# Sums and parts of v and of the weights pinned to their steps, and the first two products of the next pair ahead of the three that end the pair in work

## The chip, the cores and the metric

The kernel runs on one core of a Trainium2 chip. TensorE (PE in the profile; its weight loads are PEld) multiplies, VectorE (DVE), ScalarE (ACT) and GpSimd (POOL) work beside it, and SyncE (SP) issues all DMAs. The metric is device time in microseconds (us) of one execution. Before the change the median of three runs is 2376.45 us (2374.65 to 2376.95).

## The reference

Channel attention on q, k and v of shape (4, 6080, 256), and then a gated layer without a second input on all 4 x 6080 tokens:

```python
qn = q / (norm(q, axis=1) + 1e-06)
kn = k / (norm(k, axis=1) + 1e-06)
s = kn.transpose(0, 2, 1) @ qn / tau        # 256 x 256 for each batch
a = softmax(s)                              # exp(s - max) / (sum + 1e-09)
x = (v @ a).reshape(24320, 256)
h = x @ w_in                                # 256 x 2048
g = h * sigmoid(1.702 * h)
return g @ w_out                            # 2048 x 256
```

## The kernel before

For each batch the attention matrix is folded into the input weights, so that v is multiplied by one matrix of 256 x 2048 that is new in each batch ("the weights"). The product of v and the weights is done by Strassen's scheme in Winograd's form, with seven block products in place of eight, called P0 to P6 here after the block of weights that each uses. That needs sums of blocks of v and of the weights ahead of the products, and sums of products after them. Each fp32 operand is split into a high and a low part (`split`, L81: a cast on ACT, then a subtraction on DVE), and each product is three matmuls: high x high, high x low, low x high.

**The stream.** The tokens of a batch lie in 12 chunks of up to 512 (half a chunk is 256 columns, in the last chunk 224). A chunk meets 8 pairs of 128-row blocks of the hidden layer. One pair is one *period*; the four batches have 384 of them. `Hidden` holds a pair, and its work has three pieces:

- `begin` (L541): P0 into half of one PSUM bank (`ps_x`), P4 into half of another (`ps_y`). ACT copies P0 out (`r1`, L553), and DVE adds it to P4 (`u2`, L554).
- `middle` (L556): P5 into `ps_y` and P3 into `ps_x`. P5 has to wait until DVE has read `ps_y` for `u2`. DVE then makes `r25` (L561) and adds it in `ps_y` (L563).
- `end` (L565): P1, P6 (`ps_x`) and P2 (`ps_y`). DVE adds `u2` to both banks (L569, L570), and `gate` (L576) runs the activation `g` from each bank (ACT, L581) and splits it into `gh` and `gl` (ACT L82, DVE L83).

`project` (L592) multiplies `gh` and `gl` by the output weights, six matmuls of up to 512 columns for each of the pair's two blocks. The list `late` holds it back, so that a period projects the pair that ended one period earlier. The banks for pairs come from a pool of four (`ps_h`), so a new pair takes the banks of the pair before the last.

**Order.** In the main loop TensorE's order is written by hand (`manual_schedule` for PE, L754). A period is, in TensorE's order: `end` of the pair before, `begin` of the new pair, a `project`, the side work of step 2s, `middle`, a `project`, the side work of step 2s + 1. All other engines run in order from queues whose order a scheduler decides by its own costs, as early as data and buffers allow. `with tc.issue_after(ins)` puts ACT's instructions of a block behind `ins` in ACT's queue; work of the block on other engines follows only through its data. `pinned` (L749) does so with `newest[0]`, the `r1` of the newest pair. Before the change only the preparation of q and k (`prep`) and the first piece of each weight conversion go through it.

**Side work** is given a step (`put`, `put0`, `put_w`). In a chunk that begins at step `at_v`, for the next chunk: `v_load` (three DMAs) at `at_v` + 3, `v_sums` (four additions, on POOL after the first chunks) at `at_v` + 6, and four `v_split` at `at_v` + 8, 10, 12 and 14. The parts of v (`vh`, `vl`) have two buffers, so the parts of the next chunk go where those of the chunk before were, and are free to be written once that chunk's last product has run. For the next batch, `prepare` of a unit of q and k every 4 steps (two splits and two squares on ACT, their low parts on DVE, sums on POOL), its scores three steps later, then norms, softmax (`softmax_a`, L358, with exp on ACT, L384) and, in the last chunk and the first steps of the next batch, for each of four groups `win_load`, `win_split`, `weights` (L431), `weight_sums` and `weight_split`.

A stage of some 62 us before the main loop does batch 0's attention. In the first 160 us the weights also have to be put together from 64-bit words.

Of the kernel before, what the change touches and what calls it, by code (L numbers as in the profile page):

```python
# [27 lines left out]
def channel_attention_then_glu(  # L28
# [27 lines left out]
    NF = DFF // P  # L56
# [121 lines left out]
    class Attention:  # L178
# [98 lines left out]
        def score(self, u, qs, ks):  # L277
            nt = self.units[u][1]
            start = 0 if self.alone else self.direct
            if u == start:  # L280
                self.s = [
                    ps_s.tile([P, 2 * C], F32, tag=f"s{i}", name=f"s{i}")
                    for i in range(NC2)
                ]
            steps = [(j, i) for j in range(nt) for i in range(NC2)]
            last = u == len(self.units) - 1
            if u < self.direct:
                for j, i in steps:
                    nc.tensor.matmul(
                        self.s[i][:, :C],  # L290
                        lhsT=ks[:, j, i * P : (i + 1) * P],
                        rhs=qs[:, j, :],
                        start=u == start and j == 0,
                        stop=last and j == nt - 1,
                    )
                return

            for j, i in steps:
                nc.tensor.matmul(  # L299
                    self.s[i],  # L300
                    lhsT=ks[:, j, 0, i * P : (i + 1) * P],
                    rhs=qs[:, j, :, :],
                    start=u == start and j == 0,
                    stop=False,
                    skip_group_check=True,
                )
            for j, i in steps:
                nc.tensor.matmul(  # L308
                    self.s[i][:, C:],
                    lhsT=ks[:, j, 1, i * P : (i + 1) * P],  # L310
                    rhs=qs[:, j, 0, :],
                    start=False,
                    stop=last and j == nt - 1,
                    skip_group_check=True,
                )
# [276 lines left out]
    def project(b, c, f, gh, gl):  # L592
        o, w = chunks[c]
        if f == 0:

            room = [(ps_s, f"s{i}") if (b, c) == (0, 1) else (ps_o, "o") for i in range(NC2)]
            po[b, c] = [p.tile([P, NCH], F32, tag=t, name="ps_o") for p, t in room]
        out = po[b, c]
        for d in range(NC2):
            ds = slice(d * P, (d + 1) * P)  # L600
            for n, (l, r) in enumerate(((wo_h, gh), (wo_h, gl), (wo_l, gh))):
                nc.tensor.matmul(  # L602
                    out[d][:, :w], lhsT=l[:, f, ds], rhs=r[:, :w],
                    start=f == 0 and n == 0, stop=f == NF - 1 and n == 2,
                )
        if f == NF - 1:
            for d in range(NC2):
                osb = op.tile([P, NCH], F32, tag="osb", name="osb")[:, :w]
                if d == 0:
                    nc.vector.tensor_copy(osb, out[d][:, :w])  # L610
                else:
                    nc.scalar.copy(osb, out[d][:, :w])
                dst = outT[d * P : (d + 1) * P, b * N + o : b * N + o + w]
                nc.sync.dma_start(dst, osb)
# [10 lines left out]
    at = Attention(0, nu)  # L625
    nxt = Attention(1, 4)
# [75 lines left out]
    def put0(s, fn, *a):  # L702
        start.setdefault(s, []).append((fn, a))
# [7 lines left out]
        11: ("out", 3), 12: ("in", 6), 14: ("in", 7), 16: ("out", 4),  # L711
        18: ("out", 5), 20: ("out", 6), 22: ("out", 7),
    }
    running = {}
    newest = {}

# [17 lines left out]

    wanted = {1: 8, 2: 16, 3: 22}
    for g, n in wanted.items():
        put0(n - 5, at.win_split, g)
        for i in range(NC2):
            put0(n - 4 + i, at.weights, g, i)
        put0(n - 3, at.weight_sums, g)  # L740
        put0(n - 2, at.weight_split, g, 0)
        put0(n - 2, at.weight_split, g, 1)


    late = []
    open_ = []
    WIDE = max(begun) + 4

    def pinned(fn, *a):  # L749
        with tc.issue_after(newest[0].ins):  # L750
            fn(*a)


    with tc.manual_schedule(engines={mybir.EngineType.PE}):  # L754
        for b in range(B):
            side = start if b == 0 else carried
            following = {}
            order = [(c, f) for c in range(NCHUNK) for f in range(NF // 2)]
            if b == 0:

                beside = [(c, f) for f in range(5) for c in range(2)]
                order[:NF] = beside + [(c, f) for c in range(2) for f in range(5, NF // 2)]

            def put(s, fn, *a):
                side.setdefault(s, []).append((fn, a))

            for c in range(2 if b == 0 else 1, NCHUNK + (b + 1 < B)):
                at_v = (c - 1) * NF
                bc = (b, c) if c < NCHUNK else (b + 1, 0)
                first_v = at_v + 3  # L770
                if b == 0 and c == 2:
                    first_v = 27
                put(first_v, v_load, *bc)
                late_v = max(at_v + 6, first_v + (1 if b == 0 and c == 2 else 3))
                put(late_v, v_sums, *bc)
                for n in range(4):
                    put(at_v + 8 + 2 * n if first_v == at_v + 3 else 29 + n // 2, v_split, *bc, n)
            if b + 1 < B:
                if b:
                    nxt = Attention(b + 1)  # L780
                held = {}

                def prep(u, nxt=nxt, held=held):
                    held[u] = nxt.prepare(u)

                def score(u, nxt=nxt, held=held):
                    nxt.score(u, *held.pop(u))

                first = 2 * NF + 3 if b == 0 else 20
                nd = nxt.direct  # L790
                for u in range(nu):
                    if u < nd:
                        put(WIDE + 2 * u, pinned, prep, u)
                        continue
                    at_u = first + 4 * (u - nd)
                    put(at_u - 4, nxt.fetched, u)
                    put(at_u, pinned, prep, u)
                    put(at_u + 3, score, u)
                e = first + 4 + 4 * (nu - nd)
                put(e, nxt.norms_a)  # L800
                put(e + 4, nxt.norms_b)
                put(e + 9, nxt.norms_c)
                put(e + 10, nxt.softmax_a)
                put(e + 13, nxt.softmax_c)
                put(e + 16, nxt.transposes)
                total = NCHUNK * NF
                for g in range(NG):

                    n = total - NF + 4 * g + 5
                    there = side if n < total else following  # L810
                    n -= 0 if n < total else total

                    def put_w(s, fn, *a, there=there):
                        there.setdefault(s, []).append((fn, a))

                    put(total - NF + 4 * g - 2, nxt.win_load, g)
                    put(total - NF + 4 * g + 2, nxt.win_split, g)
                    for i in range(NC2):
                        put_w(n + i, nxt.weights, g, i)
                    put_w(n + 1, nxt.weight_sums, g)  # L820
                    put_w(n + 2, nxt.weight_split, g, 0)
                    put_w(n + 2, nxt.weight_split, g, 1)

            def sides(s):
                for fn, a in side.get(s, ()):
                    fn(*a)

            for s, (c, fp) in enumerate(order):
                if b == 0 and 2 * s == WIDE:
                    wide[0] = 1  # L830
                if open_:
                    late.extend(open_.pop().end())
                h = Hidden(at, b, c, fp)
                open_.append(h)
                h.begin()
                if len(late) > 2:
                    project(*late.pop(0))
                sides(2 * s)
                h.middle()
                if len(late) > 2:  # L840
                    project(*late.pop(0))
                sides(2 * s + 1)
            carried = following
            if b + 1 < B:
                at = nxt
        late.extend(open_.pop().end())
        while late:
            project(*late.pop(0))
# [27 lines left out]
```

## Time and profile before

| | |
|---|---|
| median of three runs | 2376.45 us |
| the profiled execution | 2376.57 us |
| its span, first to last instruction | 2374.8 us |
| mean granted TensorE clock | 0.994 |
| TensorE busy in the slice 2300 to 2374 us | 71.27 of 74 us |
| HBM over the span | 49 GB/s |

The profiled execution stands 0.1 us over the median, and 1.8 us of it lie outside the span. TensorE is busy in nearly all of the 40 slices of the span, but its matmuls overlap: a matmul of 256 columns is shown as 0.28 us long, and the next starts 0.12 us after it. So the time that TensorE loses is read from the starts of its matmuls and from the idle time ahead of its weight loads, and not from its busy share.

### The profile page before, as it was taken

How to read it: one execution, taken by the hardware profiler on the slowest of the kernel's cores; microseconds unless marked ns; L12 is line 12 of the kernel's file. 1: busy time of each engine (PE TensorE's matmuls, PEld its weight loads, DVE VectorE, ACT ScalarE, POOL GpSimd, SP SyncE). 2: the span in 40 equal slices, each digit the busy share in tenths (PEclk: the TensorE clock that was granted, in tenths of full speed). 3: DMA queues.
4: the chain of work that ended last, by engine and by line, in shares of the span. 5: the costliest groups of instructions: out<-in, count | busy, mean ns of one | idle time of the engine just before them, and what ended most of it. 6: DMA issues, size and time to landing. Idle time of an engine off the chain costs nothing.

```text
span 2374.8 us, 36966 instructions
## 1 busy us (share of the span) xinstructions
PE 2266.9 (95%) x13712; PEld 2001.5 (84%) x13712; DVE 1667.0 (70%) x3347; ACT 1329.7 (56%) x2690; POOL 390.4 (16%) x396
## 2 busy tenths in 40 slices
PE   8899999999999999999999999999999999999999
PEld 7678888878888888888888888888888888888888
DVE  7887767766667777777666777777667666666665
ACT  6666665554555666555455666565546444544544
POOL 0013322200121332220011232222002100000000
PEclk9899999999999999999999999999999999999999
DMA  8222111100011211211010111211001000100100
GB/s 325 89 80 81 63 63 60 45 25 29 28 35 36 81 63 54 70 45 35 19 36 26 63 63 56 70 34 36 27 19 36 26 28 19 36 19 19 35 10 17
DMA packets 55204, 118.77 MB, mean 50 GB/s; under 512 B 6128, under 2 KB 20976, under 8 KB 55024
## 3 DMA queue, kind: packets, MB, share of 16 engines
q1 hardware_dynamic: 55024, 116.42, 14.6%
q8 instruction: 107, 1.75, 0.3%
q14 instruction: 73, 0.60, 0.1%
HBM read 89.39 MB, written 27.00 MB: 49 GB/s over the span
## 4 chain that ended last, share of the span: by engine, by line
PE 73%; DVE 12%; ACT 10%; issue 4%; DMA 1%; SPq 0%; ACTq 0%; DVEq 0%
PE ps_o L602 33%; PE ps_x L535 19%; PE ps_y L535 14%; DVE gl L83 3%; ACT vh L82 3%; PE s L299 3%; ACT g L581 2%; PE ps_w L448 2%; DVE ps_x L569 2%; DVE u L554 1%; PE s L308 1%; DVE vl L83 1%; DVE ps_y L570 1%; DVE wl L83 1%; ACT gh L82 1%
## 5 line engine op out<-in xcount | busy, mean ns | idle before, releaser
L83 DVE TENSOR_TENSOR gl<-g,gh 128x512 fp32r<-128x512 f32 (+1 forms) x768 | 567.3, 760 | 167.2 <-ACT gh L82 162.5
L602 PE MATMUL ps_o<-gl,wo_h 128*128 128x512 f32 (+1 forms) x1536 | 605.1, 394 | 0.8 <-DVE gl L83 0.7
L602 PE MATMUL ps_o<-gh,wo_h 128*128 128x512 f32 (+1 forms) x1536 | 605.9, 394 | 0.0
L602 PE MATMUL ps_o<-gh,wo_l 128*128 128x512 f32 (+1 forms) x1536 | 597.2, 389 | 0.0
L581 ACT ACTIVATE g<-ps_x 128x512 f32<-128x512 f32 (+1 forms) x384 | 227.6, 593 | 652.0 <-DVE ps_x L569 651.5
L82 ACT CAST gh<-g 128x512 fp32r<-128x512 f32 (+1 forms) x768 | 443.7, 627 | 4.3 <-PE ps_o L602 0.7
L535 PE MATMUL ps_x<-vh,wh 128*128 128x256 f32 (+1 forms) x1536 | 435.2, 283 | 5.4 <-DVE r L561 5.1
L535 PE MATMUL ps_x<-vl,wh 128*128 128x256 f32 (+1 forms) x1536 | 434.5, 283 | 1.5 <-DVE vl L83 1.5
L535 PE MATMUL ps_x<-vh,wl 128*128 128x256 f32 (+1 forms) x1536 | 434.6, 283 | 0.7 <-DVE wl L83 0.7
L535 PE MATMUL ps_y<-vh,wh 128*128 128x256 f32 (+1 forms) x1152 | 340.9, 296 | 87.0 <-DVE u L554 77.4
L569 DVE TENSOR_TENSOR ps_x<-ps_x,u 128x256 f32<-128x256 f32 (+1 forms) x384 | 163.9, 427 | 269.0 <-PE ps_x L535 266.9
L535 PEld LDWEIGHTS ps_y<-vh,wh 128*128 128x128 f32 x1152 | 219.8, 191 | 148.9 <-DVE u L554 123.2
L602 PEld LDWEIGHTS ps_o<-gh,wo_l 128*128 128x128 f32 x1536 | 290.2, 189 | 62.1
L535 PE MATMUL ps_y<-vh,wl 128*128 128x256 f32 (+1 forms) x1152 | 325.9, 283 | 2.6 <-DVE wl L83 2.6
L535 PE MATMUL ps_y<-vl,wh 128*128 128x256 f32 (+1 forms) x1152 | 325.7, 283 | 0.2 <-DVE vl L83 0.2
L602 PEld LDWEIGHTS ps_o<-gh,wo_h 128*128 128x128 f32 x1536 | 292.7, 191 | 34.4
L602 PEld LDWEIGHTS ps_o<-gl,wo_h 128*128 128x128 f32 x1536 | 292.4, 190 | 31.9 <-DVE gl L83 1.8
L535 PEld LDWEIGHTS ps_x<-vh,wh 128*128 128x128 f32 x1536 | 293.9, 191 | 26.2 <-DVE r L561 12.1
L535 PEld LDWEIGHTS ps_x<-vl,wh 128*128 128x128 f32 x1536 | 294.2, 192 | 12.8 <-DVE vl L83 1.7
L535 PEld LDWEIGHTS ps_x<-vh,wl 128*128 128x128 f32 x1536 | 294.3, 192 | 0.9 <-DVE wl L83 0.9
L554 DVE TENSOR_TENSOR u<-ps_y,r 128x256 f32<-128x256 f32 (+1 forms) x384 | 160.5, 418 | 151.6 <-ACT r L553 150.5
L581 ACT ACTIVATE g<-ps_y 128x512 f32<-128x512 f32 (+1 forms) x384 | 231.5, 603 | 0.4 <-DVE ps_y L570 0.4
(123 smaller groups left out, 2769.8 us busy)
## 6 DMA issues: line engine op xcount, KB each, us to landing
out_T<-osb SPq DMA_DIRECT2D x88, 256.0 KB, 2.2
raw_q<-in_q SPq DMA_DIRECT2D x33, 512.0 KB, 3.6
raw_k<-in_k SPq DMA_DIRECT2D x33, 512.0 KB, 4.6
v_raw<-in_vT SPq DMA_DIRECT2D x44, 256.0 KB, 2.7
v_raw<-in_vT SPq DMA_DIRECT2D x88, 128.0 KB, 2.8
win<-win SPq DMA_DIRECT2D x16, 512.0 KB, 3.3
raw_q<-in_q SPq DMA_DIRECT2D x6, 768.0 KB, 8.8
raw_k<-in_k SPq DMA_DIRECT2D x6, 768.0 KB, 9.8
```

The costliest lines, as they stand in the source:

```text
L82: ins = nc.scalar.copy(dst_hi, src)
L83: nc.vector.tensor_tensor(dst_lo, src, dst_hi.bitcast(F32), op=ALU.subtract)
L299: nc.tensor.matmul(self.s[i], lhsT=ks[:, j, 0, i * P : (i + 1) * P], rhs=qs[:, j, :, :], start=u == start and j == 0, stop=False, skip_gro ...
L308: nc.tensor.matmul(self.s[i][:, C:], lhsT=ks[:, j, 1, i * P : (i + 1) * P], rhs=qs[:, j, 0, :], start=False, stop=last and j == nt - 1, sk ...
L448: nc.tensor.matmul(ps, lhsT=l[:, j, ci], rhs=r[:, j, :], start=n == 0, stop=n == 3 * NC2 - 1,)
L535: nc.tensor.matmul(out, lhsT=l[:, wi, :], rhs=r[:, vi, : self.hw], start=first and n == 0, stop=last and n == 2, skip_group_check=True,)
L554: nc.vector.tensor_tensor(u2, self.y[:, 1], r1, op=ALU.add)
L569: nc.vector.tensor_tensor(self.x[:, 1], self.x[:, 1], self.u2, op=ALU.add)
L570: nc.vector.tensor_tensor(self.y[:, 0], self.y[:, 0], self.u2, op=ALU.add)
L581: nc.scalar.activation(g, ps, AF.Gelu_apprx_sigmoid)
L602: nc.tensor.matmul(out[d][:, :w], lhsT=l[:, f, ds], rhs=r[:, :w], start=f == 0 and n == 0, stop=f == NF - 1 and n == 2,)
```

## The change

It has two parts. `pinned` is now also laid around `v_sums`, `v_split`, `win_split`, `weight_sums` and `weight_split` in the main loop. And `begin` of the new pair is issued ahead of `end` of the pair before it, so that a period is P0, P4 of the new pair; P1, P6, P2 of the pair before; project; P5, P3; project.

```diff
+    def pinned(fn, *a):
+        with tc.issue_after(newest[0].ins):
+            fn(*a)
+
...
-        put0(n - 5, at.win_split, g)
+        put0(n - 5, pinned, at.win_split, g)
...
-        put0(n - 3, at.weight_sums, g)
-        put0(n - 2, at.weight_split, g, 0)
-        put0(n - 2, at.weight_split, g, 1)
+        put0(n - 3, pinned, at.weight_sums, g)
+        put0(n - 2, pinned, at.weight_split, g, 0)
+        put0(n - 2, pinned, at.weight_split, g, 1)
...
-                put(late_v, v_sums, *bc)
+                put(late_v, pinned, v_sums, *bc)
                 for n in range(4):
-                    put(at_v + 8 + 2 * n if first_v == at_v + 3 else 29 + n // 2, v_split, *bc, n)
+                    put(at_v + 8 + 2 * n if first_v == at_v + 3 else 29 + n // 2, pinned, v_split, *bc, n)
...
-                    put(total - NF + 4 * g + 2, nxt.win_split, g)
+                    put(total - NF + 4 * g + 2, pinned, nxt.win_split, g)
...
-                    put_w(n + 1, nxt.weight_sums, g)
-                    put_w(n + 2, nxt.weight_split, g, 0)
-                    put_w(n + 2, nxt.weight_split, g, 1)
+                    put_w(n + 1, pinned, nxt.weight_sums, g)
+                    put_w(n + 2, pinned, nxt.weight_split, g, 0)
+                    put_w(n + 2, pinned, nxt.weight_split, g, 1)
...
+                h = Hidden(at, b, c, fp)
+                h.begin()
                 if open_:
                     late.extend(open_.pop().end())
-                h = Hidden(at, b, c, fp)
                 open_.append(h)
-                h.begin()
```

**ACT, the parts of v for one chunk of the third batch.** In these rows `vh` is the high part of v, `r1` the copy of P0, `g` the activation, `gh` its high part, and `qs`, `ks`, `sq` belong to `prepare`. Before:

```order
L553 COPY r1_14560<-ps_x_14552 128x256
L581 ACTIVATE g_14540<-ps_x_14482 128x512
L82 CAST gh_14542<-g_14540 128x512
L581 ACTIVATE g_14546<-ps_y_14483 128x512
L82 CAST gh_14548<-g_14546 128x512
L82 CAST vh_14921<-v_raw_14729 128x512 x2
L82 CAST vh_14921<-v_raw_14730 128x512
L82 CAST vh_14921<-v_raw_14730 128x256
L581 ACTIVATE g_14606<-ps_x_14552 128x512
L553 COPY r1_14626<-ps_x_14618 128x256
L82 CAST qs_14636<-raw_q_14374 128x2x256
L82 CAST ks_14637<-raw_k_14376 128x2x256
```

And now:

```order
L553 COPY r1_14888<-ps_x_14880 128x256
L82 CAST vh_14921<-v_raw_14729 128x512
L82 CAST qs_14925<-raw_q_14648 128x2x256
L82 CAST ks_14926<-raw_k_14650 128x2x256
L252 ACTIVATE sq_14931<-raw_q_14648 128x512
L252 ACTIVATE sq_14934<-raw_k_14650 128x512
L581 ACTIVATE g_14903<-ps_x_14812 128x512
L581 ACTIVATE g_14909<-ps_y_14813 128x512
L82 CAST gh_14905<-g_14903 128x512
L82 CAST gh_14911<-g_14909 128x512
L553 COPY r1_14964<-ps_x_14956 128x256
L82 CAST vh_14921<-v_raw_14729 128x512
```

The four casts of a chunk, which stood together at the chunk's start, ahead of an activation and of `r1`, stand singly now, each behind the `r1` of a period of its own, four periods into the chunk; and `r1` of the new pair stands ahead of both activations of the pair before.

**DVE, the low parts of the same v.** Here `u2` is the sum that P5 waits for, L569 and L570 finish a pair's banks, L561 and L563 follow P3. Before:

```order
L563 TENSOR_TENSOR ps_y_14553<-ps_y_14553,r25_14578 128x256
L569 TENSOR_TENSOR ps_x_14552<-ps_x_14552,u2_14561 128x256
L570 TENSOR_TENSOR ps_y_14553<-ps_y_14553,u2_14561 128x256
L83 TENSOR_TENSOR vl_14922<-v_raw_14729,vh_14921 128x512 x2
L83 TENSOR_TENSOR vl_14922<-v_raw_14730,vh_14921 128x512
L83 TENSOR_TENSOR vl_14922<-v_raw_14730,vh_14921 128x256
L554 TENSOR_TENSOR u2_14627<-ps_y_14619,r1_14626 128x256
L83 TENSOR_TENSOR qs_14636<-raw_q_14374,qs_14636 128x2x256
```

And now:

```order
L554 TENSOR_TENSOR u2_14889<-ps_y_14881,r1_14888 128x256
L83 TENSOR_TENSOR vl_14922<-v_raw_14729,vh_14921 128x512
L569 TENSOR_TENSOR ps_x_14812<-ps_x_14812,u2_14821 128x256
L570 TENSOR_TENSOR ps_y_14813<-ps_y_14813,u2_14821 128x256
L83 TENSOR_TENSOR qs_14925<-raw_q_14648,qs_14925 128x2x256
L83 TENSOR_TENSOR ks_14926<-raw_k_14650,ks_14926 128x2x256
L561 TENSOR_TENSOR r25_14947<-ps_x_14880,u2_14889 128x256
L563 TENSOR_TENSOR ps_y_14881<-ps_y_14881,r25_14947 128x256
L83 TENSOR_TENSOR gl_14906<-g_14903,gh_14905 128x512
L83 TENSOR_TENSOR gl_14912<-g_14909,gh_14911 128x512
L554 TENSOR_TENSOR u2_14965<-ps_y_14957,r1_14964 128x256
L83 TENSOR_TENSOR vl_14922<-v_raw_14729,vh_14921 128x512
```

The four subtractions stood between L570 and `u2`; now `u2` comes first in its period, one subtraction behind it, and L569 and L570 of the pair before behind both.

**ACT, the softmax for the third batch.** `ACT_TABLE_LOAD` changes between the tables of the activation and of exp; `x` and `z` are the softmax's. Before:

```order
L553 COPY r1_11716<-ps_x_11708 128x256
L581 ACTIVATE g_11696<-ps_x_11645 128x512
L581 ACTIVATE g_11702<-ps_y_11646 128x512
L82 CAST gh_11698<-g_11696 128x512
L82 CAST gh_11704<-g_11702 128x512
L384 ACT_TABLE_LOAD
L384 ACTIVATE x_11730,z_11731<-x_11730,m_11732 128x256 x2
L386 ACT_TABLE_LOAD
L386 ACTIVATE m_11732<-m_11732 128x2
L553 COPY r1_11792<-ps_x_11784 128x256
```

And now:

```order
L581 ACTIVATE g_11708<-ps_x_11622 128x512
L384 ACT_TABLE_LOAD
L384 ACTIVATE x_11730,z_11731<-x_11730,m_11732 128x256
L581 ACT_TABLE_LOAD
L581 ACTIVATE g_11714<-ps_y_11623 128x512
L384 ACT_TABLE_LOAD
L384 ACTIVATE x_11730,z_11731<-x_11730,m_11732 128x256
L82 CAST gh_11710<-g_11708 128x512
L82 CAST gh_11716<-g_11714 128x512
L386 ACT_TABLE_LOAD
L386 ACTIVATE m_11732<-m_11732 128x2
L553 COPY r1_11769<-ps_x_11761 128x256
```

An activation of the pair before now stands between the two exps, with two more table loads. The same order stood, and stands, at the softmax for the second batch; at the one for the fourth it is new, as here.

More of the change, by code (lines that the diff above doesn't have):

```diff
@@ L747, in channel_attention_then_glu @@
     WIDE = max(begun) + 4
-    def pinned(fn, *a):
-        with tc.issue_after(newest[0].ins):
-            fn(*a)
     with tc.manual_schedule(engines={mybir.EngineType.PE}):
```

## The prediction, made before the changed kernel was run

> **What bounds the kernel now.** The page's first part names the busiest engine:
>
> ```profile
> PE 2266.9 (95%) x13712; PEld 2001.5 (84%) x13712; DVE 1667.0 (70%) x3347; ACT 1329.7 (56%) x2690; POOL 390.4 (16%) x396
> ```
>
> TensorE bounds it, and no other engine is near its limit over the whole span. The change removes no matmul, so it can only win time in which TensorE stands still. The waits of TensorE and of its weight loads from 200 us to the end, and one wait of ACT over the whole span (us in total, times, longest), say for whom it stands still:
>
> ```profile
> PE ps_y L535 <- DVE u L554: 71.1, 58, 4.0
> PE ps_x L535 <- DVE r L561: 3.4, 1, 3.4
> PEld ps_y L535 <- DVE u L554: 112.4, 92, 4.4
> ACT vh L82 <- PE ps_y L535: 126.9, 46, 3.7
> ```
>
> Nearly all of it is one wait: P5 for DVE's `u2`. The last row names a cause: 46 times, about once for each chunk, ACT waits up to 3.7 us with casts of v at the head of its queue. The timeline of one chunk's start in the third batch shows the whole chain:
>
> ```profile
> 1504.53 1.97 ACT L82 CAST vh<-v_raw 128x512 fp32r<-128x512 f32 x4 [3.68 <-PE ps_y L535]
> 1505.19 2.23 DVE L83 TENSOR_TENSOR vl<-v_raw,vh 128x512 fp32r<-128x512 f32 x4 [0.22 <-ACT vh L82]
> ...
> 1505.98 0.39 PE L602 MATMUL ps_o<-gl,wo_h 128*128 128x512 f32 x1
> ...
> 1506.21 0.39 PE L602 MATMUL ps_o<-gh,wo_l 128*128 128x512 f32 x1
> 1506.41 0.59 ACT L581 ACTIVATE g<-ps_x 128x512 f32<-128x512 f32 x1
> 1506.90 0.36 ACT L553 COPY r<-ps_x 128x256 f32<-128x256 f32 x1
> 1507.15 0.63 ACT L82 CAST qs<-raw_q 128x512 fp32r<-128x512 f32 x1
> 1507.34 0.42 DVE L554 TENSOR_TENSOR u<-ps_y,r 128x256 f32<-128x256 f32 x1
> 1507.67 0.63 ACT L82 CAST ks<-raw_k 128x512 fp32r<-128x512 f32 x1
> 1507.81 0.19 PEld L535 LDWEIGHTS ps_y<-vh,wh 128*128 128x128 f32 x1 [1.63 <-DVE u L554]
> 1507.81 0.38 PE L535 MATMUL ps_y<-vh,wh 128*128 128x256 f32 x1 [1.20 <-DVE u L554]
> 1508.03 0.28 PE L535 MATMUL ps_y<-vl,wh 128*128 128x256 f32 x1
> 1508.15 0.28 PE L535 MATMUL ps_y<-vh,wl 128*128 128x256 f32 x1
> ```
>
> All four casts of v run as soon as the old parts are read out, an activation and `r1` stand behind them, `u2` stands behind `r1`, and P5 comes 1.2 us late.
>
> What a stop costs: projections start 0.23 us apart (1505.98, 1506.21), but this P5 starts 1.60 after the last of them, 1.37 late, and its second matmul follows after 0.22 in place of 0.12, 0.10 more. That is 1.47, where PEld's row shows 1.63, so a wait of PEld overstates by 0.16. From 200 us on the waits for `u2` cost 112.4 - 92 x 0.16 = **98 us**.
>
> **The change, part by part.** A period without a stop, from its P1 to the next one's P1, is this:
>
> ```profile
> 1541.23 0.28 PE L535 MATMUL ps_x<-vh,wh 128*128 128x256 f32 x1
> ...
> 1542.31 0.28 PE L535 MATMUL ps_x<-vh,wh 128*128 128x256 f32 x1
> ...
> 1543.12 0.37 ACT L553 COPY r<-ps_x 128x256 f32<-128x256 f32 x1
> 1543.37 0.63 ACT L82 CAST qs<-raw_q 128x512 fp32r<-128x512 f32 x1
> 1543.52 0.42 DVE L554 TENSOR_TENSOR u<-ps_y,r 128x256 f32<-128x256 f32 x1 [0.57 <-ACT r L553]
> ...
> 1544.42 0.28 PE L535 MATMUL ps_y<-vh,wh 128*128 128x256 f32 x1
> ...
> 1546.52 0.28 PE L535 MATMUL ps_x<-vh,wh 128*128 128x256 f32 x1
> ```
>
> It lasts 5.29. P0 starts at 1542.31, `u2` ends at 1543.94, P5 comes at 1544.42: a slack of 0.48.
>
> *The new order.* P1, P6 and P2 (1541.23 to 1542.31, 1.08 us) move from before P0 to between it and P5, so P5 comes 3.19 after P0 and the slack is 1.56. Also `r1` and `u2` now stand ahead of the old pair's activations and last sums. This alone is over the 1.47 of the stop above.
>
> *The pinned casts.* Each of a chunk's four casts now stands behind a period's `r1`, so each delays activations by one ACT step of 0.52 (1507.15 to 1507.67) instead of four at once.
>
> *What is late next* is the activation: `begin` of the next period takes the banks of the old pair. Take the fullest period, with a cast of v and a unit of q and k, counted from P0. `r1` starts at 0.7 (P0's third matmul starts at 0.24, is 0.28 long, and 0.19 passes), the next ACT row 0.25 later, then five steps (`vh`, `qs`, `ks`, two squares) of 0.52: the activation of `ps_x` starts at 3.6, that of `ps_y` ends at 4.7. P4 of the next period wants the second bank at 5.29 + 0.36 = 5.65: 0.95 us of slack. On DVE a 512-wide subtraction is at most
>
> ```profile
> L83 DVE TENSOR_TENSOR gl<-g,gh 128x512 fp32r<-128x512 f32 (+1 forms) x768 | 567.3, 760 | 167.2 <-ACT gh L82 162.5
> ```
>
> 0.76 long in the mean. Behind `u2` (to 1.6) stand `vl` 0.6, four sums like `u2` (L569, L570, L561, L563) of 0.42 and four subtractions of 0.76: done by 7.0, the next `u2` by 7.4, and P5 comes at 3.19 + 5.29 = 8.5. So no stop is left in an ordinary period, and I book all of the 98, except at three places.
>
> *The softmax.* ACT at the second batch's softmax, where the order is as it will be at all three, and TensorE at the third batch's:
>
> ```profile
> 498.74 1.28 ACT L384 ACT_TABLE_LOAD   x1
> 500.04 0.51 ACT L384 ACTIVATE x<-x,m 128x256 f32<-128x256 f32 x1
> ...
> 506.80 0.20 ACT L386 ACTIVATE m<-m 128x2 f32<-128x2 f32 x1
> ...
> 1092.35 0.39 PE L535 MATMUL ps_y<-vh,wh 128*128 128x256 f32 x1 [0.77 <-DVE z L391]
> ```
>
> From the load to `m`'s end are 8.26 us, with the activation ahead (0.6) 8.9. In the new period that activation starts at about 2.1 (P6, then L569), so the next `r1` starts at 11.0 and `u2` ends at 11.9, where P5 was due at 8.5: a stop of 3.4 and about 0.3 for the restart. Today the second batch's has one of the same size (3.4, for L561 in the list of waits), the third's one of 0.77, and so, I take it, the fourth's. Net 2 x 2.7 = **+5** (0 to +8).
>
> The Trainium skill ("ScalarE: Activation LUTs", section What ACT_TABLE_LOAD costs) gives a switch of tables 1.28 us for the load and some 1.38 more for a drain. Here the exp starts 0.02 after its load's end, so this trace agrees with the load and shows no drain.
>
> *The weights.* At each group of weights DVE splits `win` and `wf` ahead of `u2`:
>
> ```profile
> 1238.90 1.81 DVE L83 TENSOR_TENSOR win_l<-win,win_h 128x1024 fp32r<-128x1024 f32 x1
> 1240.93 1.45 DVE L83 TENSOR_TENSOR wl<-wf,wh 128x1024 fp32r<-128x1024 f32 x1
> 1242.61 0.37 DVE L554 TENSOR_TENSOR u<-ps_y,r 128x224 f32<-128x224 f32 x1
> 1243.04 0.37 PE L535 MATMUL ps_y<-vh,wh 128*128 128x224 f32 x1 [1.02 <-DVE u L554]
> ```
>
> P5 stops for 1.02, with the restart some 1.2. In the new queue the two splits are still ahead of `u2`, with L569 moved behind it, and P5 has 1 us more; what is left I take between nothing and today's 1.2, half, at three groups of three batches: **+5** (0 to +11). The longest stops, of 4.0 us, just ahead of 675, 1260 and 1843, where v's four casts ran into the weights' splits, go.
>
> *The clock.* After those three stops the granted clock sags (PE, PEld, DVE, ACT, POOL, then the clock, by stretch):
>
> ```profile
> 675.00:678.00 3.00, 2.94 (x13) 2.71 (x14) 1.93 (x5) 0.00 (x0) 1.15 (x2) 0.68 0.26 82
> 1260.00:1263.00 3.00, 3.00 (x11) 2.83 (x12) 1.63 (x4) 0.00 (x0) 1.42 (x2) 0.50 0.20 64
> 1843.00:1846.00 3.00, 2.97 (x11) 2.80 (x12) 1.90 (x4) 0.00 (x0) 1.15 (x2) 0.57 0.29 91
> 505.00:508.00 3.00, 2.95 (x15) 2.95 (x16) 2.86 (x8) 2.24 (x4) 0.00 (x0) 0.57 0.00 0
> ```
>
> 3 x (0.32 + 0.50 + 0.43) = 3.8, and about 1 more in the stretches behind: **-5**. The last row is the softmax at 505, 1.3 lost; the softmax stops may now do so three times, in pieces: **+2** (-1 to +3).
>
> The Trainium skill ("TensorE: Matmul & The Clock Gate", section Part 1: The HAM clock gate) says that an idle window of some 3.4 us halves TensorE's clock; the rows above, behind stops of 3.4 to 4.0 us, agree. By it each new softmax stop would be dearer, which is inside the bounds.
>
> *The first 160 us.* There DVE is the bound:
>
> ```profile
> 120.00:140.00 20.00, 17.72 (x100) 14.69 (x99) 19.22 (x40) 14.70 (x28) 0.00 (x0) 1.00 0.24 85
> ```
>
> DVE works 19.22 of 20 us and its work stays, so I book **-3** (-8 to +3).
>
> *POOL and SP.* The pins act on ACT alone, so POOL's sums move only by their data; v's sums (step 6) have a period or more before the cast that needs them. v's loads go behind q's and k's on SP and land in
>
> ```profile
> v_raw<-in_vT SPq DMA_DIRECT2D x44, 256.0 KB, 2.7
> ```
>
> 2.7 us, with a period and a half to spare. If that cover went, ACT would wait in its queue with the activations behind it. I book nothing.
>
> Sum: -98 + 5 + 5 - 5 + 2 - 3 = **-94**. From the profiled execution's 2376.57 (0.1 over the median) that is 2282.6, so about **2282 us**. With all bounds the good way -112 (2265), the other way -78 (2299).
>
> **The rivals.**
> *Half comes back*: the regular stops at the chunk starts go, but half of the 98 returns as waits for a bank that an activation still reads, or for `gl`, in the fuller periods. For it: 0.95 us of slack is not much for queues that were set by a scheduler's costs. Against it: the slack was worked out at the fullest period, and most have neither a cast of v nor a unit of q and k. 2282.6 + 49 = 2332.
> *The activation becomes the bound, slower than before*: `begin` waits at P4 for the bank that ACT still reads, behind `prepare`. About 75 periods prepare a unit (25 for each of three batches). To eat up 94 us, each must stop 1.25 us, so the activation must end 0.95 + 1.25 = 2.2 us later than worked out; from there on the change loses. At 2.6 it gives 2282.6 + 75 x 1.65 = 2406. Against it: ACT's steps in such a period (0.25, five of 0.52, two activations of 0.5, two casts of 0.6) sum to 5.1 of 5.29 us, and the scores that follow in the next period give TensorE more work and ACT none.
> *It doesn't do what it says*: the scheduler could have put the casts back together. The rows of the new order show them apart, so the time would stay at 2376 only if `u2` were held by something that the profile doesn't name.
> *A drain at each table switch* (the skill's rule above): if each of five switches at a softmax held ACT 1.38 us longer, 3 x 6.9 = +21, 2303. The 0.02 us between load and exp speak against it.
>
> **How the numbers follow.** The forecast, 2265 to 2299: 0.80. Half comes back: 0.10. The drain: 0.02. No change: 0.03. Slower: 0.05. The range 2262 to 2318 holds the forecast (and 3 us below it, for short waits that aren't listed here), the drain, and the better edge of the half case. A measurement of this kernel tells about 0.2% (4.8 us) from no change. Faster by more 0.92, within it 0.03, slower 0.05.
>
> **What would show it.** Right: TensorE's waits for `u2` under 10 us; ACT's wait of `vh` for `ps_y` gone; v's casts single; no stop at the chunk starts. For the new places: stops of some 3.7 us at each of three softmaxes, up to 1 us at weight groups. Wrong: waits of `ps_x` or `ps_y` for ACT's `g` in periods with `qs` and `ks`, of `ps_o` for `gl`, or of `vh` for POOL.

## The result, and the profile after

The changed kernel takes 2273.52 us in the median of three runs (2271.59 to 2274.23), against 2376.45 before: a ratio of 0.9567 (95% interval 0.9545 to 0.9589), or -103 us. The profiled executions differ by 105 us (2376.57 and 2271.59); the prediction had booked -94.

The first part of the changed kernel's page:

```profile
PE 2231.9 (98%) x13712; PEld 2003.0 (88%) x13712; DVE 1685.7 (74%) x3347; ACT 1349.2 (59%) x2694; POOL 423.8 (19%) x396
```

The work is the same on TensorE; ACT has four table loads more. The waits of TensorE and of its weight loads from 200 us to the end (us in total, times, longest):

```profile
PE ps_y L535 <- DVE u L554: 6.7, 12, 0.7
PE ps_y L535 <- ACT g L581: 3.7, 3, 1.2
PE ps_o L602 <- ACT gh L82: 2.2, 3, 0.7
PE ps_o L602 <- DVE gl L83: 2.0, 3, 0.7
...
PEld ps_y L535 <- DVE u L554: 12.3, 15, 1.1
```

TensorE's wait for `u2` fell from 71.1 us in 58 times to 6.7 in 12. Each of the three rows below it has three entries, one for each softmax; the first two are new, and the third had two short entries (0.7 us) before. ACT's wait of `vh` for `ps_y` (126.9 us before) is gone from the list.

The timeline of a period of the third batch that has both a cast of v and a unit of q and k, the fullest kind, and the period behind it:

```profile
1419.81 0.28 PE L535 MATMUL ps_x<-vh,wh 128*128 128x256 f32 x1
...
1420.37 0.37 ACT L553 COPY r<-ps_x 128x256 f32<-128x256 f32 x1 [1.57 <-PE ps_x L535]
...
1420.63 0.62 ACT L82 CAST vh<-v_raw 128x512 fp32r<-128x512 f32 x1
...
1422.91 1.56 POOL L254 TENSOR_TENSOR acc_q<-acc_q,sq 128x512 f32<-128x512 f32 x1 [8.74 <-ACT sq L252]
1422.99 0.28 PE L535 MATMUL ps_y<-vh,wh 128*128 128x256 f32 x1
1423.23 1.78 DVE L83 TENSOR_TENSOR ks<-raw_k,ks 128x512 fp32r<-128x512 f32 x1
...
1423.73 0.60 ACT L581 ACTIVATE g<-ps_y 128x512 f32<-128x512 f32 x1
...
1425.09 0.28 PE L535 MATMUL ps_x<-vh,wh 128*128 128x256 f32 x1
...
1425.45 0.28 PE L535 MATMUL ps_y<-vh,wh 128*128 128x256 f32 x1
...
1427.25 0.41 DVE L554 TENSOR_TENSOR u<-ps_y,r 128x256 f32<-128x256 f32 x1
...
1428.27 0.28 PE L535 MATMUL ps_y<-vh,wh 128*128 128x256 f32 x1
```

The rows at 1419.81 and 1425.09 are two P0s, 5.28 apart: no stop. The cast stands alone behind `r1`. The activation of `ps_y` ends at 1424.33, 4.52 after P0 (the prediction: 4.7), and P4 takes the next bank at 1425.45, so 1.12 us are left (0.95). But `u2` of the next period ends at 1427.66, 0.61 ahead of P5 at 1428.27, where the prediction left 1.1: `ks` took 1.78 us, not 0.76, while POOL added squares.

The timeline of the third batch's softmax:

```profile
1038.59 0.60 ACT L581 ACTIVATE g<-ps_y 128x512 f32<-128x512 f32 x1
1039.20 1.28 ACT L384 ACT_TABLE_LOAD   x1
...
1039.24 0.39 PE L535 MATMUL ps_y<-vh,wh 128*128 128x256 f32 x1 [1.24 <-ACT g L581]
...
1041.66 0.49 PE L602 MATMUL ps_o<-gh,wo_h 128*128 128x512 f32 x1 [0.73 <-ACT gh L82]
...
1042.81 0.50 PE L602 MATMUL ps_o<-gl,wo_h 128*128 128x512 f32 x1 [0.66 <-DVE gl L83]
...
1044.42 0.39 PE L535 MATMUL ps_y<-vh,wh 128*128 128x256 f32 x1 [0.16 <-DVE u L554]
```

The stop comes in four pieces. By starts of matmuls against their usual distance they cost 1.39, 0.89, 0.92 and 0.35 us, 3.55 in all, and the same at the other two batches. The clock stays full there (columns as in the prediction):

```profile
1039.00:1045.00 6.00, 4.21 (x23) 3.12 (x23) 3.22 (x9) 5.57 (x11) 0.00 (x0) 1.00 0.00 0
1595.00:1602.00 7.00, 4.53 (x25) 3.46 (x26) 3.55 (x10) 6.56 (x12) 0.00 (x0) 1.00 0.01 2
```

**Where the 105 us came from.** Summing over all matmuls what their distance to the next start exceeds the median for their kind, TensorE loses 37.9 us in the first 200 us and 113.7 behind them before the change, and 31.2 and 20.2 after it. That is 100 of the 105, starts at a halved clock included. The other 5 lie in the medians themselves: the next matmul starts 231 ns behind a projection of 512 columns, of which there are 4224, where it was 232, and 203 behind the 383 of 448 columns, where it was 205. Why, no run shows. Of the 20.2 left, 10.7 are the softmaxes, and 8.4 are nine stops of 0.74 to 0.89 at the weights, with 0.1 of restart each.

### The profile page after: what moved, and what is told of

The parts are those of the page before. It is cut to its first block, busy times and chain, and to the rows that moved or that the text cites. A ratio compares the mean times of both kernels' runs of the same rounds, so it can differ in the third digit from the quotient of the medians.

```text
span 2269.8 us, 36869 instructions
## 1 busy us (share of the span) xinstructions
PE 2231.9 (98%) x13712; PEld 2003.0 (88%) x13712; DVE 1685.7 (74%) x3347; ACT 1349.2 (59%) x2694; POOL 423.8 (19%) x396
## 3 DMA queue, kind: packets, MB, share of 16 engines
q8 instruction: 107, 1.75, 0.3%
## 4 chain that ended last, share of the span: by engine, by line
PE 91%; DVE 4%; ACT 3%; issue 2%; DMA 1%; SPq 0%; DVEq 0%; ACTq 0%
PE ps_o L602 44%; PE ps_x L535 23%; PE ps_y L535 17%; PE s L299 3%; PE ps_w L448 2%; PE s L308 1%; PE s L289 1%; DMA raw_k<-in_k 1%; DVE u L554 0%; DVE gl L83 0%; DVE win_l L83 0%; ACT sq L252 0%; DVE acc_k L254 0%; ACT L384 0%; DVE wl L83 0%
## 5 line engine op out<-in xcount | busy, mean ns | idle before, releaser
L82 ACT CAST gh<-g 128x512 fp32r<-128x512 f32 (+1 forms) x768 | 438.2, 623 | 1.9
L553 ACT COPY r<-ps_x 128x256 f32<-128x256 f32 (+1 forms) x384 | 142.8, 372 | 415.8 <-PE ps_x L535 415.8
L535 PE MATMUL ps_y<-vh,wh 128*128 128x256 f32 (+1 forms) x1152 | 328.6, 285 | 17.4 <-DVE u L554 7.0
L561 DVE TENSOR_TENSOR r<-ps_x,u 128x256 f32<-128x256 f32 (+1 forms) x384 | 159.2, 415 | 120.7 <-PE ps_x L535 120.6
```

The source lines that it names most:

```text
L82: ins = nc.scalar.copy(dst_hi, src)
L535: nc.tensor.matmul(out, lhsT=l[:, wi, :], rhs=r[:, vi, : self.hw], start=first and n == 0, stop=last and n == 2, skip_group_check=True,)
L553: newest[0] = nc.scalar.copy(r1, self.x[:, 0])
L561: nc.vector.tensor_tensor(r, self.x[:, 1], self.u2, op=ALU.add)
```

## The experiments

Medians below are of four runs each; the kernel before, run beside them, had medians of 2374.6 to 2379.3 in the different jobs, so ratios to it are given too.

**Each part alone.** The new order with the five added `pinned` taken out:

```diff
-                put(late_v, pinned, v_sums, *bc)
+                put(late_v, v_sums, *bc)
...
-                    put(at_v + 8 + 2 * n if first_v == at_v + 3 else 29 + n // 2, pinned, v_split, *bc, n)
+                    put(at_v + 8 + 2 * n if first_v == at_v + 3 else 29 + n // 2, v_split, *bc, n)
```

(and the same for `win_split`, `weight_sums` and `weight_split`).

> The new order of products without the added pins. Theory (P5's slack is what counts, 0.48 us before and 1.56 with the new order): the casts of v stand together again, but behind r1 and u2, so that the 1.47 us stops at P5 go; four casts (1.97 us) now stand ahead of the old pair's activations, which end some 0.5 us after P4 of the next period wants their bank, in the chunks that also prepare q and k. About 2300 us (2285 to 2315). Rival (the pins are what counts): 2340 us or more.

2299.0 us, ratio 0.9666 (0.9652 to 0.9681): as expected. Its weight loads wait 19.3 us for `u2` from 200 us on, in place of 112.4, though ACT still runs the casts four in a row, at each of 44 chunks. What it has beyond the changed kernel is mainly 9.6 us of waits for DVE's sum L563 (14 times), 5.8 for `gl` (12) and 4.0 for the activation of `ps_x` (10). And all pins, with `end` ahead of `begin` as before:

```diff
-                h = Hidden(at, b, c, fp)
-                h.begin()
                 if open_:
                     late.extend(open_.pop().end())
+                h = Hidden(at, b, c, fp)
                 open_.append(h)
+                h.begin()
```

> The pins with the old order of products. Theory: the regular stops at the chunk starts go (44 x 1.47 = 65 us) and the three of 4 us with their sagging clock; the slack of P5 stays 0.48, so the short waits for u2 stay. About 2303 us (2285 to 2320), and TensorE's weight loads still wait for u2 some 30 to 45 us. Rival (the order is what counts): 2340 us or more.

2322.0 us, 0.9758 (0.9743 to 0.9772), slower than expected. Its weight loads' waits from 200 us on:

```profile
PEld ps_y L535 <- DVE u L554: 36.0, 66, 1.4
PEld ps_o L602 <- DVE gl L83: 24.0, 24, 1.2
```

The waits for `u2` fell as expected, but project waits 24 times for `gl`, in the kernel before 2 times and in the changed one 3. So the parts, -57 and -79 by their ratios, don't add up to the whole, -103.

**Which pin.** Only `v_split` pinned, once in the new order and once in the old:

> The changed kernel with only v_split pinned; sums of v, sums and parts of the weights and win_split without. Theory: the pins on the other work do nothing that counts, since the sums run on POOL and the weights' parts are held by their data: 2273 us, within 5. Rival (the weights' pins hold the longest stops away): 2285 us or more.

> Only v_split pinned, with the old order of products. Theory: the same as all pins with the old order, within 5 us, about 2303. Rival (the weights' pins count where the slack is small): 10 us or more slower than all pins with the old order.

2272.79 us (0.9555, 0.9541 to 0.957) and 2320.58 (0.9751, 0.9735 to 0.9768): the same as with all pins, so the 2303 expected for the old order was missed here too. The other four pins do nothing that can be measured.

**Why the pins alone give back 20 us.** The timeline at one of the 24 places:

```profile
723.33 1.28 POOL L254 TENSOR_TENSOR acc_k<-acc_k,sq 128x512 f32<-128x512 f32 x1
...
723.62 1.54 DVE L83 TENSOR_TENSOR gl<-g,gh 128x512 fp32r<-128x512 f32 x1
...
725.22 0.50 PE L602 MATMUL ps_o<-gl,wo_h 128*128 128x512 f32 x1 [0.66 <-DVE gl L83]
```

This `gl` lasts 1.54 us. It starts inside an addition of POOL that ends at 724.61, and ends 0.55 behind that. All 24 last 1.54 to 1.79 us, each beside an addition of k's squares. Left out, to see it, are POOL's additions of the squares of q and k for batches 2 to 4; what stands behind them, the norms too, still runs, on sums that lack them:

```diff
-                    eng = nc.vector if self.alone else nc.gpsimd
-                    eng.tensor_tensor(acc, acc, sq, op=ALU.add)
+                    if self.alone:
+                        nc.vector.tensor_tensor(acc, acc, sq, op=ALU.add)
```

> The kernel with all pins and the old order (2322.0 us, 24 new waits of project for gl), but POOL's additions of the squares of q and k for the batches after the first are left out, with the norms that hang on them. Theory, the collision: in the timeline of the kernel with the pins alone, a subtraction gl at 723.62 takes 1.54 us in place of 0.69 while POOL adds squares (723.33 to 724.61), and ends 0.55 after POOL does. If this is what makes project wait, the 24 waits for gl go (under 2 us in all) and the time falls by 24 x (0.66 + 0.16) = 20 us, to about 2302 (2297 to 2306). Rival, the later r1: r1 comes 1.08 us later in the old period, and what is pinned behind it pushes gl back whatever POOL does; then the 24 waits stay, some shorter, and the time is 2314 to 2322.

> The changed kernel (2273.5 us) with the same additions on POOL left out. There 61 subtractions of k's low part stretch to 1.67 us beside POOL in place of 0.69, but no stop of TensorE is seen in those periods. By the collision theory the new order has room for it, so the time stays within 2 us of 2273.5 and only the subtractions get shorter (mean under 0.75 us). Rival, the new order also pays a little in each of some 67 periods that prepare: 2262 to 2268.

> The kernel before with the same additions on POOL left out, to close the square: with them the pins alone are worth 2376.5 - 2322.0 = 54 us. Theory: in the kernel before the stops come from four casts of v in a row on ACT, which POOL has no part in; only some 20 us of its stops have a subtraction stretched by POOL in the 3.5 us ahead, most of those behind the casts too. So the time falls by 4 (start) to 20 us, to 2355 to 2372, likeliest 2365, and without POOL the pins are worth 2365 - 2284 = 81 us: what they lack of that with POOL, some 27 us, is what the collisions take back. Rival: POOL's collisions cost the old queues as much as the pinned ones, so the kernel before gains 35 us or more too: 2341 or less, and the pins are worth 54 with POOL or without.

| | with POOL's additions | without | ratio without |
|---|---|---|---|
| before | 2376.45 | 2354.46 | 0.9906 (0.9889 to 0.9923) |
| pins alone | 2322.0 | 2283.58 | 0.9614 (0.9599 to 0.9628) |
| the changed kernel | 2273.52 | 2269.14 | 0.9555 (0.9541 to 0.9569) |

In each of the three rows the queues of ACT and DVE hold the same instructions in the same order with the additions and without, so nothing else was moved by leaving them out.

With the pins alone the additions cost 38 us by the medians and 34 by the ratios, nearly twice the 20 expected. The weight loads' waits of that kernel without them:

```profile
PEld ps_y L535 <- DVE u L554: 22.4, 41, 1.4
PEld ps_x L535 <- DVE r L561: 11.1, 15, 3.8
PEld ps_y L535 <- DVE ps_y L563: 4.9, 6, 1.0
```

All 24 waits for `gl` are gone, which settles it against the later `r1`; and 25 of the 66 waits for `u2` go too, which the expectation had not counted. What it is about the pinned queues that brings `gl` beside the additions was not tried. The kernel before loses 22 us to them, just past the upper end expected; of its 92 waits for `u2`, 58 are left without them:

```profile
PEld ps_y L535 <- DVE u L554: 92.9, 58, 4.4
```

The changed kernel loses 4, more than the 2 expected, though the intervals of the two ratios overlap; it lies nearly all in the first 580 us, in gaps too short to show as stops. Behind 200 us one stop of 0.25 us goes and two of 0.23 fall to 0.16; the others stay within 0.03. Yet the collisions are as long there as ever, and more: 198 of its 512-wide subtractions from 200 us on last over 0.8 us, in the kernel before 90. `ks` on DVE in the changed kernel from 200 us on, and then without the additions (duration in ns, lowest, median, highest):

```profile
L83 DVE TENSOR_TENSOR ks<-raw_k,ks x69: 628/1667/1793, 206.3 to 1540.6; 128x512 fp32r<-128x512 f32 x63, 128x256 fp32r<-128x256 f32 x6
```

```profile
L83 DVE TENSOR_TENSOR ks<-raw_k,ks x69: 412/684/1085, 204.5 to 1536.8; 128x512 fp32r<-128x512 f32 x63, 128x256 fp32r<-128x256 f32 x6
```

So the new order does not avoid the collisions, it has room for them: in the period shown above, P5 1.08 us earlier, as in the old order, would have stood 0.47 us for `u2`. By ratios without POOL's additions the pins are worth 69 us (81 were expected) and the order, on top of them, 14; with the additions, 57 and 45. Of the change's 103 us, 83 would be there without these additions, and some 20 are collisions with them that no longer reach TensorE. POOL's sums of v and of the weights stay in all these runs: without the additions 66 subtractions of the changed kernel still last over 0.8 us, and what those cost was not tried.

**Is the activation near to being the bound?** Two, then four extra copies on ACT in every period, behind `r1` (their output is used by nothing):

```diff
+            with tc.issue_after(newest[0].ins):
+                for _ in range(2):
+                    nc.scalar.copy(idle, wo_l[:, 0, 0:P].bitcast(F32))
```

> The changed kernel with two more copies of 128 columns on ACT in each period, behind r1 (their output is used by nothing). Theory (0.95 us of slack of the activation in the fullest period): the copies take some 0.4 us together, no stop in ordinary periods; only the 3 softmax stops and the weights' get longer: 2273 to 2280 us. Rival (ACT is all but the bound): 75 periods and more each stop by 0.4, 2300 us or more.

> Four such copies, some 0.8 us a period. Theory: still inside the slack of 0.95 but for the fullest periods, those after a softmax and at the weights: 2276 to 2290 us. Rival (ACT is all but the bound): 2330 us or more. If the activation's slack is as worked out, TensorE's first new waits are those of ps_y for ACT's g.

Two copies: 2279.29 us (0.9589, 0.9574 to 0.9603), inside the expected range. Four: 2267.4 (0.9534, 0.9518 to 0.955), faster than the changed kernel and outside it. TensorE's waits for the activation from 200 us on with two copies, and then with four, whose lines are shifted (L585 is the activation):

```profile
PE ps_y L536 <- ACT g L585: 3.5, 3, 1.2
```

```profile
PE ps_y L536 <- ACT g L585: 2.3, 2, 1.2
```

They stay at the softmaxes, so ordinary periods bear the four copies, of 0.23 us busy each (ACT 1529.4 us with two, 1349.2 without, 768 copies). The times, though, do not follow from the copies' cost. The scheduler made other queues elsewhere: with two copies the third weight stop of each batch grew from 0.74 to 2.2 us; with four, three stops of 1.66 us that the changed kernel has near 99, 127 and 148 us are gone, and so is most of the second batch's softmax stop. As a measure of slack in us this is inconclusive; that the activation isn't the bound in ordinary periods, it shows.

**The stops that are left.** exp of the softmax held in ACT's queue behind the newest activation (for the second batch a period later):

```diff
-            nc.scalar.activation(g, ps, AF.Gelu_apprx_sigmoid)
+            gated[0] = nc.scalar.activation(g, ps, AF.Gelu_apprx_sigmoid)
...
+    def behind_gate(fn, *a):
+        with tc.issue_after(gated[0].ins):
+            fn(*a)
...
-                put(e + 10, nxt.softmax_a)
+                put(e + 10 + (b == 0), behind_gate, nxt.softmax_a)
```

> The changed kernel with the softmax's exps put behind the newest activation in ACT's queue (one step later for the second batch's), so that the two exps follow each other with one table load. Theory (the stops of 3.6 us at each softmax are ACT's, from the activation that stands between the exps with two more table loads): the chain from the activation to the next r1 shortens by some 3.3 us; most of the 3 x 3.6 goes: 2264 us (2261 to 2269). Rival (they come from DVE's work or from the exps themselves): no change, 2273.

2269.38 us (0.9545, 0.9531 to 0.956), about half of what was expected. The second batch's stop fell to 0.8, the others only to 1.94, because there both casts to `gh` now stand behind the exps, and project waits for them. Then also each split of `win` a period later (`4 * g + 4` for `4 * g + 2`). In this kernel that leaves out the split of the last group for batches 2 to 4, whose last weights are then made from the group before it:

> As the run with the exps behind the newest activation, and win_split two steps later, so that DVE has the subtraction of win (1.8 us) behind u2 and not ahead of it. Theory: the nine stops of some 0.9 us at the weight groups come from the two long subtractions ahead of u2; they go as well: 8 us less than that run, 2256 us (2251 to 2262). Rival (the stops are held by the next thing, the group's wf and POOL's sums): the same as that run.

2263.96 us (0.9523, 0.9508 to 0.9537), 2 us outside the range expected, with those splits left out. Two of each batch's three weight stops are gone, and the third falls to 0.5. Last, the version that does all the work: the exps behind the newest `gh` in place of the activation, and the last group's split in the next batch's first period:

```diff
-            split(gh[:, :w], gl[:, :w], g)
+            gated[0] = split(gh[:, :w], gl[:, :w], g)
...
-                put(e + 10, nxt.softmax_a)
+                put(e + 10 + 2 * (b == 0), behind_gate, nxt.softmax_a)
...
-                    put(total - NF + 4 * g + 2, pinned, nxt.win_split, g)
+                    at_w = total - NF + 4 * g + 4
+                    if at_w < total:
+                        put(at_w, pinned, nxt.win_split, g)
+                    else:
+                        following.setdefault(at_w - total, []).append((pinned, (nxt.win_split, g)))
```

> The changed kernel with exp of the softmax put in ACT's queue behind the newest gh that is issued by then (for the second batch one period later), and each split of win one period later, the last group's in the first period of the next batch; all work is done. The softmax stops should fall from 3.55 to about 1 at each of three places (-7.7), the weight stops from 2.5 to 0.5 for each of three batches (-6): 2260 (2256 to 2266). If ACT's work at the softmax only moves into the activations of the next pair, the softmax stops stay at 2 or more and the time is 2264 or above.

2260.96 us (2258.27 to 2261.94), ratio 0.9518 (0.9502 to 0.9534): as expected, and below both kernels. Its third batch's softmax:

```profile
1037.83 0.62 ACT L82 CAST gh<-g 128x512 fp32r<-128x512 f32 x1
1038.35 0.59 ACT L581 ACTIVATE g<-ps_y 128x512 f32<-128x512 f32 x1
1038.96 1.28 ACT L384 ACT_TABLE_LOAD   x1
...
1041.77 0.36 ACT L553 COPY r<-ps_x 128x256 f32<-128x256 f32 x1
...
1042.66 1.28 ACT L386 ACT_TABLE_LOAD   x1
...
1043.92 0.39 PE L535 MATMUL ps_y<-vh,wh 128*128 128x256 f32 x1 [1.39 <-DVE u L554]
```

Both exps run behind the activation with one load, and the load back stands behind `r1`. One stop is left, 1.54 by starts, at the third and fourth batches, and none over 0.3 at the second.

## Why the prediction was right, and where it was off

- **The bound and the cause: right.** The waits for `u2` at the chunk starts were the loss, and four casts in a row ahead of `r1` their cause: the pin of `v_split` alone takes the regular stops of 1.4 us at the chunk starts away, and so does the new order alone, in which they still stand four in a row.
- **The new order's 1.08 us: right, and worth more than was said.** The prediction took the slack of 1.56 as more than enough for a stop of 1.47. The runs show a second use: it covers subtractions stretched by POOL's additions of squares, which were 22 us of the loss before, of which the prediction says nothing.
- **DVE's queue: the step that failed, without effect on the sign.** "On DVE a 512-wide subtraction is at most 0.76 long in the mean" took a mean over two kinds: 0.68 to 0.69 alone and up to 1.79 beside POOL. So the slack of `u2` in the fullest period was 0.6 and not 1.1. That this left the forecast standing was luck: the 1.08 us were booked against stops behind the casts, and happen to be as long as the stretch. For the pins alone, where they are missing, the same step put the expectation 19 us off, and the rival's waits for `gl` are there.
- **ACT's queue: right.** 4.52 for 4.7 us; the rival in which the activation becomes the bound has no wait to show outside the softmaxes.
- **The softmax: the size right, the place wrong.** Booked was one stop of 3.7 at P5, for `u2`; 3.55 came in four pieces, the first at P4 for the activation that stands between the exps. Net of the stops of before (3.55 and twice 0.93) it is +5.2, for +5.
- **The weights: mis-sized.** Nine places at half of today's 1.2 gave +5; they measured 0.93 each, 8.4 in all. The first of them:

```profile
613.22 1.81 DVE L83 TENSOR_TENSOR win_l<-win,win_h 128x1024 fp32r<-128x1024 f32 x1
614.03 1.60 POOL L464 TENSOR_TENSOR wf<-wf 128x256 f32<-128x256 f32 x1
614.95 1.75 DVE L83 TENSOR_TENSOR wl<-wf,wh 128x1024 fp32r<-128x1024 f32 x1
...
616.63 0.38 DVE L554 TENSOR_TENSOR u<-ps_y,r 128x224 f32<-128x224 f32 x1
...
617.07 0.37 PE L535 MATMUL ps_y<-vh,wh 128*128 128x224 f32 x1 [0.73 <-DVE u L554]
```

  With `win`'s split a period later two of three go. But that move does two things. It takes one split out of the period's DVE queue, and it takes it from beside POOL's sums of the weights: `win_l` and `wl` last 1.81 and 1.75 us here, 1.21 and 1.60 there, and 1.21 to 1.23 each in the first 150 us. Beside POOL they are 1.1 us longer, more than the stop. No run leaves these sums out, so which of the two makes the stop stays open.
- **The clock: right for the sag, the wrong sign at the softmax.** Before, slow starts in the stretches at half clock behind the three long stops cost 4.7 us (5 booked), and those behind the second batch's softmax 1.4. All four stretches are gone, so the term of +2 measured -1.4. The softmax stretches above and those just behind the weights' third stops show a granted clock of 1.00:

```profile
645.00:651.00 6.00, 6.00 (x36) 5.44 (x35) 3.89 (x9) 4.19 (x11) 0.74 (x1) 1.00 0.00 0
1199.00:1205.00 6.00, 5.38 (x32) 4.63 (x32) 4.75 (x9) 3.55 (x8) 1.82 (x2) 1.00 0.28 90
1755.00:1761.00 6.00, 5.38 (x31) 4.59 (x30) 5.41 (x10) 3.03 (x8) 2.20 (x2) 1.00 0.00 0
```

  A stop's length alone doesn't settle whether the clock sags: with the new order alone a stop of 2.47 us at 484 us was followed by 3.4 us at a clock of 0.50, with the pins alone one of 3.55 us at 490 us by none (1.00).
- **The first 160 us: -3 booked,** -1 at 142 us and -5 at 187 us measured by the projections' starts, within the bounds.
- **What was not booked:** short waits for L561 and L563. In the kernel before the weight loads' rows from 200 us on are

```profile
PEld ps_x L535 <- DVE r L561: 8.7, 21, 3.8
PEld ps_y L535 <- DVE ps_y L563: 8.7, 31, 1.0
```

and now 0.3 (1 time) and 0.8 (5). Without the softmax's 3.8 and 0.16 for each of the others, that is some 5 us. Behind 200 us 93.5 were won. The terms as measured give 98 - 5.2 - 8.4 = 84.4; with these 5 and the 6.1 of the clock it is 95.5, so 2 us more than was won.

The rival of a drain at each table switch is out: the switches cost what their loads last, and the stop came out under 3.7.

## What to carry to other kernels

Side work that a scheduler may start as early as data allow gathers where buffers come free, ahead of what the bound engine waits for; tying each piece behind the newest instruction of the chain, a period apart, was worth 59 us here by itself, with one line (the pin of `v_split`). Moving work of the bound engine in between a producer chain and its consumer was worth more where the other engines are less regular, 45 us on top of the pins with POOL's additions and 14 without: look at the longest of a group of instructions and not at the mean, and ask which engine runs beside the long ones. Two parts of a change are not to be added up until each has been run alone.

## What the runs showed of the hardware

Of the DVE instructions of the main loop, those with both inputs in SBUF collide with POOL's additions, and which of the two starts first decides who pays. In the changed kernel from 200 us on, 193 subtractions of 512 columns began inside an instruction of POOL that had more than 0.3 us to go: all took over 0.8 us, up to 1.79, and as a rule ended 0.55 behind POOL's end. The 30 that began ahead of one took 0.68. Then it is POOL's that lasts longer: its additions of squares 1.74 us in the median where they began inside a subtraction, 1.29 where they didn't. DVE's sums with an operand in PSUM don't stretch, though 64 to 102 of each of L561, L563, L569 and L570 ran beside POOL for at least 0.1 us. In the changed kernel from 200 us on:

```profile
L569 DVE TENSOR_TENSOR ps_x<-ps_x,u x365: 381/425/433, 199.7 to 2260.9; 128x256 f32<-128x256 f32 x167, 128x224 f32<-128x224 f32 x16
L570 DVE TENSOR_TENSOR ps_y<-ps_y,u x365: 381/423/433, 200.0 to 2261.3; 128x256 f32<-128x256 f32 x167, 128x224 f32<-128x224 f32 x16
```

The Trainium skill ("SBUF — State Buffer", section Who interferes with whom) states this rule: a DVE instruction with two inputs in SBUF and a GpSimd instruction that reads SBUF shut each other out, and the later one waits for the whole of the other. This trace agrees both ways, with 0.68 against up to 1.79 us on DVE and 1.29 against 1.74 on POOL, and with the two rows above, which stay under 0.44.
